# Two banks in two tiles: batch 0's numerators apart from their divisors, and another order of work

## The chip, the cores and the metric

The kernel runs on one core of one Trainium2 chip. The metric is device time in microseconds. The time before is 284.9 us, the median of three runs (284.8, 284.9 and 285.23).

## What is computed

The reference is a linear attention followed by a two-layer feed-forward block:

```python
# q, k, v: (8 batches, 8 heads, 576 positions, 64)
theta = pi / 2 * pos / 576
phi(x) = concat([relu(x) * cos(theta), relu(x) * sin(theta)], -1)   # 64 -> 128 features
q_p, k_p = phi(q), phi(k)
kv  = einsum('bhsf,bhsd->bhfd', k_p, v)          # 128 x 64 for each head
z   = sum(k_p, axis=2)                           # 128 for each head
num = einsum('bhsf,bhfd->bhsd', q_p, kv)
den = einsum('bhsf,bhf->bhs', q_p, z)[..., None] + 1e-06
x   = (num / den).transpose(0, 2, 1, 3).reshape(4608, 512)
h   = x @ w_in                                   # (512, 2048)
out = (relu(h) ** 2) @ w_out                     # (2048, 512) -> (4608, 512), float32
```

## The kernel before

Inputs are cast to bf16 as they are loaded. The 576 positions of a batch are cut into four blocks of 128 (j = 0 to 3) and a tail of 64 (j = 4). The tails of all eight batches are gathered and make up a ninth unit of the feed-forward block, so there are units u = 0 to 8: unit u is batch u, and unit 8 is the tails.

**Attention of a batch b.** `features` makes the feature rows of k and q (operations kf, qf, kqf). `values` copies v beside a column of ones (vc, vct), so that one product gives kv and z together. `kv` sums over the positions into the two banks of psA (operations kz), and the result is copied to `kvz` (8 heads x 65 columns, the 65th being z). q's features are transposed, by TensorE for batches 0 to 2 (tq, copied out by tqc), by a DMA for the others (qT on SyncE's queue). `numerators` multiplies q's transposed features with kvz (num): 8 products of 65 columns, four heads in each of two banks. Then den adds 1e-6 to the 65th column of each head, and div takes its reciprocal on VectorE and multiplies the 64 others with it, reading PSUM. x is transposed, by TensorE for batches 0 to 2 (tx, txc) and by DMA for the others (xT).

**Feed-forward of a unit u.** Units 0 and 1 do the first product plainly (G, evicted by a relu r, squared by sq), unit 0 the second one too (H, evicted by y0). From unit 2 on (from unit 1 on in the second product) a product of 2 x 2 blocks is done as seven products with sums of blocks in place of eight. In the first product (`first_seven`, four parts i for each unit) they are called P1 to P7 and go to the banks X, Y and E; their evictions are c1, cu and cv (copies of partial results), r11 and r21 (relu on either engine), and r22 and r12 (add and relu, line 829, always VectorE). In the second product (`second_seven`, and `last_seven` for unit 8) they are Q1 to Q7 and go to the banks X2, Y2 and E2: Q1 and Q2 sum in X2; Q5 and Q3 in E2; Q6, Q7 and Q4 in Y2. Between them stand the evictions d1 (X2 copied to Y2), y11 (out of X2), du and dv (out of Y2), y22 (E2 plus a part kept aside, line 961, VectorE), y21 (out of Y2), y12 (E2 plus another part, line 961). The sums of blocks of g (s1 to s4, `gsums`) and of x (t1 to t4) are VectorE's. One operation P or Q is four matmuls of 256 columns.

**PSUM.** There are eight banks of 512 float32 a partition. X, Y, E and Y2 are a tile each. psA is one tile of two banks, and so is psB, whose halves are called X2 and E2:

```python
bank = {n: psum.tile([P, FP], F32, name="ps" + n) for n in ("X", "Y", "E", "Y2")}
psA = psum.tile([P, 2, FP], F32, name="psA")
psB = psum.tile([P, 2, FP], F32, name="psB")
bank["X2"], bank["E2"] = psB[:, 0, :], psB[:, 1, :]
```

Batch 0's numerators alternate between the pairs psB (j = 0 and 2) and psA (j = 1 and 3); all later numerators go to psA. The transposes tq0.0 and tq0.2 go to X2 and E2, tq0.1 and tq0.3 to X and Y; those of batches 1 and 2 to psA.

**The order.** `plan.add` registers 1405 operations with keys of what they read and write; X2 and E2 have separate keys there. `TABLE` lists the operations by number, in the order in which they are issued; each engine runs its own in that order. A "+" gives an operation to the second engine that it may run on (of VectorE and ScalarE), and "a<b" holds the load a until operation b is done. The framework puts in the semaphores between engines by the tiles that an instruction reads and writes. `FILL` gives the sizes of groups of matmuls on zeros, into bank E, that stand in the opening: 11, 1, 4 and 1 (operations 1401 to 1404), besides 28 such matmuls at the start (warm). Loads are issued by GpSimd's queue, stores and DMA transposes by SyncE's.

Of the kernel before, what the change touches and what calls it, by code (L numbers as in the profile page):

```python
# [11 lines left out]
F32 = mybir.dt.float32  # L12
# [3 lines left out]
FP = 512  # L16
# [76 lines left out]
FILL = (11, 1, 4, 1)  # L93
TABLE = """
# [9 lines left out]
212 206+ 211 248 213 214 243 276 249 284 283 278+ 286 215 254 216 279 244+ 318<279 239 255 288  # L104
285+ 250 319<244 289 294 287 320<289 291 292+ 298 240+ 261 295+ 251+ 299+ 290 245 360 300+ 293+
357 257 362 321<357 301 297 219 364 303+ 302 296+ 224 246 322<302 247+ 304 323<224 230 306
324<304 305 225 325<305 307 326<225 226+ 252 309+ 308 361 220 253 363 256+ 310 259 311 365 312
313 258+ 314 221 315 260+ 316 262 263 227 317+ 476+ 266 479 480 474+ 477 233 475 473 264 234 478
265+ 267+ 495<478 327 270 328 329 272 271 332 273 235 333 486 334 485+ 236 483 484 337 481 237
268 366 338+ 339 330 269 231 359 274+ 342 335 331 487 371 343 344 372 373 232 368 374 336+ 340  # L110
347 482+ 345 348 381 349 375 488 496<348 382 341+ 369 383 497<382 346+ 350 489 498<350 351+ 490
409 491 413 410 499<409 492 412 414 493 358 376 500<412 494 418 411 501<358 416 370 419 384 417
502<416 420 385 415 503<420 421 504 428 422 423 386 505 424 506 425 429 377 426 378 507 427 431
508+ 433 432 387 509 434 388 389 367 510 435 390 627 443 436 631 430 633 630+ 511 629 438 437
391 439 392 512 635 628 444 440 513 393 640 394 632 448 395 441 514 446 449 396 379 447 515 450
516 380 403 451 397 442 517 634+ 445 453 452 458 454 649<442 518 636 398 639 459 637 399 650<398
638+ 463 651<399 461 519+ 464 455 652<461 520 404 462 456 465 653<404 643 457+ 466+ 644 654<643
645 646 655<466 460 468 467 567 656<468 469 563 405 568 564 406 657<405 565 470 566 572 471 647
# [4 lines left out]
788 612 671 606 538 613 672 787 533 791+ 539 803<787 615 609 616 551 550 617 673 674 552 618 553  # L123
534+ 675 721 792 619 790 789 557 620 793 717 804<789 554 718 797 805<554 555 622 720 798 610
806<622 623 558 559 611 722 807<610 560 614 808<560 799 621 726 724 719 727 624 561 725 800 625
728 562 736 729 556 626 801 723 795 802 731 676 679 732 680 737 681 796 730 682 678 812 683 739
733 740 813 741 814 694 742 695 734 696 735 743 815 744 738 809<815 751 816+ 817 746 810<751 684
747 745 811<746 685 818 752 686 677 687 819 688 754 820 821 756 697 757 755+ 748 698 822 749 758
823+ 699 824 759 689 936+ 753 944 825 942 761 941 943+ 766 937 826 762 938 690 950 760 691 767
692 827 750+ 940 763 828 771 935 769 764 948 700 772 770+ 701 702 693 773 703 875 774 704 833  # L130
768 939 776 775 949 705 777 946 706 947 876 871 778 872 711 945+ 779 712 957<711 713 765 780+
714 958<713 880 959<714 874 707 873 878 960<707 881 708 830 879 951 961<708 952 709 882 962<952
831 953 883 954 955 963<954 890 956 832 885 964<890 877 886 966 715 834 891 835 884 967+ 716 836
968 895 965<836 837 893 896 887 894 843 888 969 897 970 889+ 971 892 838 898+ 844 972 848 899
# [34 lines left out]
def kernel(  # L169
# [9 lines left out]
    nc = tc.nc  # L179
# [22 lines left out]
    psum = ctx.enter_context(tc.tile_pool(name="psum", bufs=1, space=bass.MemoryType.PSUM))  # L202

    def sb(name, shape, dt=BF16):
        return const.tile(shape, dt, name=name)


    bank = {n: psum.tile([P, FP], F32, name="ps" + n) for n in ("X", "Y", "E", "Y2")}
    psA = psum.tile([P, 2, FP], F32, name="psA")
    psB = psum.tile([P, 2, FP], F32, name="psB")  # L210
    bank["X2"], bank["E2"] = psB[:, 0, :], psB[:, 1, :]

    def as_bf(ap, n):

# [80 lines left out]
    def pe(t):  # L295
        return [("PE", t, t)]
# [242 lines left out]
    def numerators(b, j, banks="A"):  # L539
        src = qpT[j // 2][:, j % 2] if j < J else qptT  # L540
        kz = kvz[b % 2]

        ps, key = (psA, [("A",)]) if banks == "A" else (psB, [("X2",), ("E2",)])

        def mm():
            for hh in range(HH):
# [696 lines left out]
```

## Time and profile before

| | |
|---|---|
| median of the runs | 284.9 us |
| the profiled execution | 286.38 us |
| its span, first to last instruction | 284.6 us |
| mean granted TensorE clock | 0.997 |
| TensorE busy | 271.1 us, 2904 matmuls recorded |
| VectorE busy | 223.2 us, 430 instructions |
| ScalarE busy | 180.4 us, 290 instructions |
| DMA, mean over the span | 132 GB/s; the loads of batch 7 land by 177 us |

TensorE's busy time counts a matmul until its modelled end, which overlaps the start of the next: four matmuls of 256 columns are recorded with 0.60 us, and the next four start 0.436 us after them. A row of the timeline gives the start, the length, the engine, the line, what is written and read, the number of instructions, and in brackets the idle time of the engine before it and what ended that. Both banks of psB carry the name psB there.

### The profile page before, as it was taken

How to read it: one execution, taken by the hardware profiler on the slowest of the kernel's cores; microseconds unless marked ns; L12 is line 12 of the kernel's file. 1: busy time of each engine (PE TensorE's matmuls, PEld its weight loads, DVE VectorE, ACT ScalarE, POOL GpSimd, SP SyncE). 2: the span in 40 equal slices, each digit the busy share in tenths (PEclk: the TensorE clock that was granted, in tenths of full speed). 3: DMA queues.
4: the chain of work that ended last, by engine and by line, in shares of the span. 5: the costliest groups of instructions: out<-in, count | busy, mean ns of one | idle time of the engine just before them, and what ended most of it. 6: DMA issues, size and time to landing. Idle time of an engine off the chain costs nothing.

```text
span 284.6 us, 7089 instructions
## 1 busy us (share of the span) xinstructions
PE 271.1 (95%) x2904; PEld 228.7 (80%) x2911; DVE 223.2 (78%) x430; ACT 180.4 (63%) x290; POOL 58.8 (21%) x89
## 2 busy tenths in 40 slices
PE   8999999999899999999999999999999899999992
PEld 2579767867679798889897989799888788888882
DVE  0766888968889869999999879969779766776941
ACT  3756767789766787775577865755556368745220
POOL 8924164441070080014020530000000000000000
PEclk9999999999999999999999999999999999999998
DMA  8999989996979599999999799544321020300134
GB/s 190 188 207 191 196 112 180 202 175 117 198 97 153 111 111 224 212 182 120 267 129 150 114 176 156 112 85 167 114 39 74 2 84 2 147 2 0 76 109 114
DMA packets 82416, 37.62 MB, mean 132 GB/s; under 512 B 51664, under 2 KB 80336, under 8 KB 82384
## 3 DMA queue, kind: packets, MB, share of 16 engines
q0 software_dynamic: 42240, 17.83, 51.5%
q1 hardware_dynamic: 39504, 18.81, 27.6%
q10 hardware_dynamic: 640, 0.52, 0.7%
q8 instruction: 23, 0.38, 0.5%
q14 instruction: 9, 0.07, 0.1%
HBM read 36.70 MB, written 9.44 MB: 162 GB/s over the span
## 4 chain that ended last, share of the span: by engine, by line
PE 80%; DVE 12%; ACT 4%; issue 2%; DVEq 0%
PE psB L940 16%; PE psY L787 10%; PE psY L940 10%; PE psE L787 7%; PE psX L787 7%; PE psB L891 4%; PE psX L733 3%; PE psA L470 3%; PE psE L733 3%; PE psA L554 3%; PE psY L733 2%; PE psY L1014 2%; DVE rt L829 2%; PE psX L1093 2%; PE psE L1093 2%
## 5 line engine op out<-in xcount | busy, mean ns | idle before, releaser
L940 PEld LDWEIGHTS <-gT 128*128 128x128 bf16 x448 | 42.8, 98 | 8.5 <-issue 3.6
L787 PEld LDWEIGHTS <-w 128*128 128x128 bf16 x448 | 42.6, 98 | 4.8
L940 PEld LDWEIGHTS <-gs 128*128 128x128 bf16 x336 | 32.6, 98 | 6.4 <-issue 2.6
L787 PEld LDWEIGHTS <-w1s 128*128 128x128 bf16 x336 | 32.3, 98 | 3.8
L787 PE MATMUL psX<-xT,w 128*128 128x256 bf16 x224 | 33.6, 273 | 0.0
L787 PE MATMUL psY<-ts,w 128*128 128x256 bf16 x224 | 33.6, 273 | 0.0
L940 PE MATMUL psB<-w,gT 128*128 128x256 bf16 x224 | 30.4, 273 | 2.6 <-DVE ysb L961 1.8
L704 ACT ACTIVATE gT<-rt 128x2048 bf16<-128x2048 bf16 x15 | 28.7, 1911 | 5.6 <-DVE rt L829 5.4
L698 ACT ACTIVATE rt<-psY 128x512 bf16<-128x512 f32 x33 | 19.7, 597 | 16.4 <-PE psY L787 13.5
L702 DVE TENSOR_TENSOR gT<-rt 128x2048 bf16<-128x2048 bf16 x21 | 25.7, 1223 | 1.6 <-ACT rt L698 0.4
L733 PEld LDWEIGHTS <-w 128*128 128x128 bf16 x320 | 25.3, 98 | 2.0
L829 DVE CUSTOM_DVE_ANT_0 rt<-psE,p1u 128x512 bf16<-128x512 f32 x28 | 19.2, 686 | 8.5 <-PE psE L787 8.4
L698 ACT ACTIVATE rt<-psX 128x512 bf16<-128x512 f32 x34 | 20.4, 601 | 7.4 <-PE psX L787 3.7
L829 DVE CUSTOM_DVE_ANT_0 rt<-psE,p1v 128x512 bf16<-128x512 f32 x28 | 19.2, 687 | 6.9 <-PE psE L787 3.4
L571 DVE TENSOR_TENSOR x<-psA,rden 128x512 bf16<-128x512 f32 x30 | 20.7, 691 | 1.9
L336 POOL DMA_DIRECT2D kqin<-in_k_dram x7 | 6.5, 922 | 71.8 <-ACT psY L399 19.2
L399 ACT COPY p1v<-psY 128x512 f32<-128x512 f32 x24 | 14.1, 586 | 10.5 <-PE psY L787 10.4
L399 ACT COPY p1u<-psY 128x512 f32<-128x512 f32 x23 | 13.5, 586 | 9.4 <-PE psY L787 9.4
L399 ACT COPY psY<-psX 128x512 f32<-128x512 f32 (+1 forms) x27 | 15.2, 563 | 4.4 <-DVE rt L696 2.7
L940 PE MATMUL psB<-w2t,gs 128*128 128x256 bf16 x112 | 15.5, 273 | 1.7 <-DVE psY L399 0.8
L787 PE MATMUL psE<-ts,w1s 128*128 128x256 bf16 x112 | 16.8, 273 | 0.0
L787 PE MATMUL psE<-xT,w1s 128*128 128x256 bf16 x112 | 16.8, 273 | 0.0
(153 smaller groups left out, 550.0 us busy)
## 6 DMA issues: line engine op xcount, KB each, us to landing
out_dram<-ysb SPq DMA_DIRECT2D x16, 512.0 KB, 3.5
kqin<-in_q_dram POOLq DMA_DIRECT2D x8, 512.0 KB, 7.5
kqin<-in_k_dram POOLq DMA_DIRECT2D x7, 512.0 KB, 6.5
vin<-in_v_dram POOLq DMA_DIRECT2D x7, 512.0 KB, 7.6
w<-in_moe_w_in_dram POOLq DMA_DIRECT2D x4, 512.0 KB, 11.7
w<-in_moe_w_out_dram POOLq DMA_DIRECT2D x4, 512.0 KB, 9.6
ysb<-in_k_dram SPq DMA_DIRECT2D x1, 1024.0 KB, 5.7
kqint<-in_k_dram POOLq DMA_DIRECT2D x16, 32.0 KB, 5.5
```

Source lines behind the costliest of these rows:

```text
L399: (nc.vector.tensor_copy if e == "DVE" else nc.scalar.copy)(out=dst, in_=src)
L470: nc.tensor.matmul(out=psA[:, half, hh * E1 : (hh + 1) * E1], lhsT=lhsT, rhs=rhs, start=(j == 0 and hh == 0), stop=(j == js[-1] and hh == ...
L571: nc.vector.tensor_tensor(out=x.rearrange("p (b k) (l d) -> p b k l d", b=n, l=2), in0=n4[:, :, :, 0:D].rearrange("p b (k l) d -> p b k l ...
L698: nc.scalar.activation(out=dst, in_=src, func=ACTF.Relu)
L702: nc.vector.tensor_tensor(out=dst, in0=src, in1=src, op=ALU.mult)
L704: nc.scalar.activation(out=dst, in_=src, func=ACTF.Square)
L733: nc.tensor.matmul(out=bank[bk][:, hh * W + c0 : hh * W + c1], lhsT=w1[:, kb, (h0 + hh) * P : (h0 + hh + 1) * P], rhs=x_block(u, t, kb)[:, ...
L787: nc.tensor.matmul(out=acc[:, hh * W : (hh + 1) * W], lhsT=lhs[:, kk, c : c + P], rhs=rhs(kk), start=start and hh == 0 and kk == 0, stop=T ...
L829: nc.vector._custom_dve(dve_ops.TENSOR_ADD_SAT, out=dst, in0=wide(acc), in1=wide(part), s0=INF, s1=0.0)
L891: nc.tensor.matmul(out=bank[bk][:, :], lhsT=g[:, hb, tt_ * P : (tt_ + 1) * P], rhs=w2[:, hb, :], start=(hb == 0), stop=True, skip_group_ch ...
L940: nc.tensor.matmul(out=acc[:, pr * W : (pr + 1) * W], lhsT=lhs[:, hb, pr * P : (pr + 1) * P], rhs=rhs[:, hb, :], start=start and pr == 0 a ...
L1093: nc.tensor.matmul(out=bank[("X", "E")[i % 2]][:, :], lhsT=zeros[:, 0:P], rhs=zeros[:, :], start=True, stop=True,)
```

## The change

X2 and E2 become tiles of their own, like the other banks, and psB is gone. Batch 0's numerators j = 0 and 2 are laid out otherwise: X2 holds the 8 x 64 numerators and E2 the 8 divisors, by 16 products in place of 8 (`mm_apart`, with the heads in order 0 to 7; before, heads 0, 4, 1, 5 and so on). den reads E2 alone, and div reads X2 alone. The planner's cost of these two operations is set to 0.5 us. The first fill has 8 matmuls in place of 11, the second 2 in place of 1, the third stays at 4, and the fourth is gone. The table of order is a new one of 1404 operations: nearly every operation is at another place, 133 of them (features, evictions, squares, dens) change between VectorE and ScalarE, and 38 of the 45 held loads are held by another operation.

```diff
-FILL = (11, 1, 4, 1)
+FILL = (8, 2, 4)
 TABLE = """
-0 1 2 3 4 6 5 7 8 9 24 10 17 22+ 25 19 23+ 11 20 12 16+ 18+ 13 21+ 14 1401 29 33+ 39 15 44 28+
-43 38 26 34 30 50 27 35 32+ 48 87 1402 37 31+ 51 52 36+ 53 40 49 88 41+ 42 54 55 45 56 57+ 46+
...
+0 1 2 3 4 6 5 7 8 9 10 17+ 19 18 22+ 25 11 21 12 16+ 23 20 24+ 13 14 1401 33+ 34 29 15 38 43+ 39
+35 28 26 44+ 30 37 27 36 50+ 1402 48 32+ 87 31+ 51 52 53 40 49 88 41+ 42 54 55 45 56 57+ 46+ 58
...
-    bank = {n: psum.tile([P, FP], F32, name="ps" + n) for n in ("X", "Y", "E", "Y2")}
+    bank = {n: psum.tile([P, FP], F32, name="ps" + n) for n in ("X", "Y", "E", "X2", "Y2", "E2")}
     psA = psum.tile([P, 2, FP], F32, name="psA")
-    psB = psum.tile([P, 2, FP], F32, name="psB")
-    bank["X2"], bank["E2"] = psB[:, 0, :], psB[:, 1, :]
...
-        ps, key = (psA, [("A",)]) if banks == "A" else (psB, [("X2",), ("E2",)])
+        key = [("A",)] if banks == "A" else [("X2",), ("E2",)]
...
+        def mm_apart():
+
+            for h in range(H):
+                for dst, cs in (
+                    (bank["E2"][:, h : h + 1], slice(D, E1)),
+                    (bank["X2"][:, h * D : (h + 1) * D], slice(0, D)),
+                ):
+                    nc.tensor.matmul(out=dst, lhsT=src[:, h, :], rhs=kz[:, h, cs], start=True, stop=True)
...
-        add(f"num{b}.{j}", pe(0.243 if j < J else 0.251), lambda e: mm(), rd, key, at=at_att(b, NUM0 + NUM1 * j))
+        go, t = (mm, 0.243 if j < J else 0.251) if banks == "A" else (mm_apart, 0.5)
+        add(f"num{b}.{j}", pe(t), lambda e: go(), rd, key, at=at_att(b, NUM0 + NUM1 * j))
...
-        n4 = ps[:, 0:n, 0 : HH * E1].rearrange("p b (h e) -> p b h e", e=E1)
+        if banks == "A":
+            n4 = psA[:, 0:n, 0 : HH * E1].rearrange("p b (h e) -> p b h e", e=E1)
+            nx, nd = n4[:, :, :, 0:D], n4[:, :, :, D]
+        else:
+            nx = bank["X2"][:, :].rearrange("p (b h e) -> p b h e", b=n, e=D)
+            nd = bank["E2"][:, 0:H].rearrange("p (b h) -> p b h", b=n)
```

More of the change, by code (lines that the diff above doesn't have):

```diff
@@ L92 @@
 ORDER2 = 'kvq23'
-FILL = (11, 1, 4, 1)
+FILL = (8, 2, 4)
 TABLE = """
[9 rows of a table removed]
[L104 to L118, printed above, removed]
[4 rows of a table removed]
-788 612 671 606 538 613 672 787 533 791+ 539 803<787 615 609 616 551 550 617 673 674 552 618 553
-534+ 675 721 792 619 790 789 557 620 793 717 804<789 554 718 797 805<554 555 622 720 798 610
@@ L125 @@
[L125 to L134, printed above, removed]
[26 rows of a table removed]
[9 rows of a table added]
+206+ 248 211 279+ 213 214 243 249 281 282 215 360 254 244 278 216+ 283 284+ 250 318<278 288 289+
+239 291 319<288 292 293+ 251+ 320<292 298 295+ 240+ 257 300+ 290 294 299+ 245 255+ 321<294 286+
@@ new lines @@
+301 246+ 287+ 261 303+ 285 296 302+ 219 297 362 322<297 247+ 304 364 323<362 252 306 324<364 361
+224 258 325<252 363 305+ 220 365 253+ 307 326<365 230 309+ 256 308+ 259 221 262+ 310 260 263 311
+312 313 314 315 478 316 266 477 481+ 476 317 233 473 479 267 474 234 264 480 265+ 475 327 272
+495<475 328 329 270 366 332 271 235 333 486 334 483+ 236 273 337 237 268 338 339 485+ 335 269
+330 359 371 274+ 342 331 231 343 487 344 225 336+ 368 372 232 373 226 340 345 484 482+ 347 227
+367 374 341+ 381 488 496<374 348 349 346+ 382 497<381 369 375 383 350 498<382 489 351+ 490 491
@@ new lines @@
+409 413 499<491 410 492 358 414 376 500<492 377 412 501<358 411 418 370 416 419 502<418 493 384
+417 503<493 420 494 385 415 421 504 386 505+ 422 423 506 428 424 425 429 387 426 388 433 427 507
+434 431 389 508 432 509 435 390 443 630 436 510 511 628 430 512+ 629 438 631 391 439 627 392 513
+640 444 393 394 437 448 395 632 514 446 449 633 440 396 515+ 447 450 516 397 451 398 441 517 378
+453 442 458 454 445 634 459 403 452 649<634 404 636+ 638 463 635+ 637 518 639 455 464 519
+650<639 520 399 461 651<399 456 465 462+ 652<461 457+ 379 466+ 405 653<462 460 380+ 643 654<460
@@ new lines @@
+468 467 567 655<468 469 563 406 564 568 644 656<406 470 566 565 645 657<566 572 407 570 573 471
[4 rows of a table added]
+534 607 609 608 671 551 610 613 552 787 553 789+ 793 617 792 803<787 791+ 790 538 618+ 615
+804<538 550 679 616 805<618 619 539 614 806<619 620 672 721 621 673+ 807<539 622 717 554 808<621
+623 718 557 720 722 624 674 558 611+ 625 559 675 726 626 797 724 795 727 798 799 719 725 800 801
+560 802 728 561 723 729 736 555 730 812 731 813+ 556 680 814 732 796 733 737 681 676 682 562 741
+683 815 678 739 742 684 816+ 740 809<739 743 677 689 744 810<743 690 734 691 811<690 746 735 751
[3 rows of a table added]
@@ L161 @@
+768 945+ 875 871 827 776 947 775 707 777 828 833 876 872 778 708 874 873 880 709 779 712 957<880
+881 713 780 714 958<713 882 959<714 878 830 883 951 960<878 952 879 953 954 832 955 961<954 885
+956 962<955 890 886 831 877 963<832 966 891 834 967+ 884 835 964<966 836 715 895 965<836 837 968
[27 rows of a table added]
 """
@@ L547, in mm @@
                 for half in range(2):
-                    e0 = hh * E1
+                    h, e0 = half * HH + hh, hh * E1
                     if j < J:
-                        dst, lhsT = ps[:, half, e0 : e0 + E1], src[:, half * HH + hh, :]
+                        dst, lhsT = psA[:, half, e0 : e0 + E1], src[:, h, :]
                     else:
                         p0, p1 = half * TAIL, (half + 1) * TAIL
-                        dst, lhsT = ps[p0:p1, 0, e0 : e0 + E1], src[:, hh, p0:p1]
-                    nc.tensor.matmul(
-                        out=dst, lhsT=lhsT, rhs=kz[:, half * HH + hh, :], start=True, stop=True
-                    )
+                        dst, lhsT = psA[p0:p1, 0, e0 : e0 + E1], src[:, hh, p0:p1]
+                    nc.tensor.matmul(out=dst, lhsT=lhsT, rhs=kz[:, h, :], start=True, stop=True)
+        def mm_apart():
[5 more added lines that the diff above has]
+                    nc.tensor.matmul(out=dst, lhsT=src[:, h, :], rhs=kz[:, h, cs], start=True, stop=True)
         rd = [("qpT", j), ("qpT", j, 0), ("qpT", j, 1), ("kvz", b % 2)]
@@ L572, in div @@
                 out=x.rearrange("p (b k) (l d) -> p b k l d", b=n, l=2),
-                in0=n4[:, :, :, 0:D].rearrange("p b (k l) d -> p b k l d", l=2),
+                in0=nx.rearrange("p b (k l) d -> p b k l d", l=2),
                 in1=rd_[:, 0:n]
@@ L581, in plus_eps @@
         def plus_eps(e):
-            src = n4[:, :, :, D]
+            src = nd
             if e == "DVE":
```

78 rows, old and new, of the table TABLE are left out of this document.

## The prediction

> **What bounds the kernel now.** I read the page's first and fourth parts, then the stretches, then the tile view of psB, then the timeline of each place where TensorE stood still.
>
> ```profile
> PE 271.1 (95%) x2904; PEld 228.7 (80%) x2911; DVE 223.2 (78%) x430; ACT 180.4 (63%) x290; POOL 58.8 (21%) x89
> PE 80%; DVE 12%; ACT 4%; issue 2%; DVEq 0%
> 120.00:140.00 20.00, 20.00 (x230) 17.66 (x229) 19.06 (x36) 13.94 (x21) 4.27 (x6) 1.00 1.09 193
> ```
>
> TensorE (PE) carries 80% of the chain that ended last. In the third line (a stretch of 20 us; busy PE, PEld, DVE, ACT, POOL) PE never idles although VectorE (DVE) works 19.06 of 20 us. So the time is PE's work plus PE's pauses, and a pause is worth its full length. The tile view of psB says who ends pauses before its instructions:
>
> ```profile
>   DVE ysb L961: 2.6, 5
>   ACT psY L399: 1.3, 3
>   ACT ysb L399: 1.1, 3
>   DVE psY L399: 0.8, 1
> ```
>
> L961 is y12 and y22, which read bank E2; psY L399 is d1 and ysb L399 is y11 or y0, most of which read X2. Next to the order of work, the timeline shows which bank PE was about to write:
>
> ```profile
> 155.19 0.69 DVE L961 TENSOR_TENSOR ysb<-psB,p2v 128x512 f32<-128x512 f32 x1
> 155.94 0.60 PE L940 MATMUL psB<-w,gT 128*128 128x256 bf16 x4 [0.53 <-DVE ysb L961]
> ...
> 222.01 0.70 DVE L399 COPY psY<-psB 128x512 f32<-128x512 f32 x1 [0.26 <-PE psB L940]
> 222.76 0.60 PE L940 MATMUL psB<-w2t,gs 128*128 128x256 bf16 x4 [0.79 <-DVE psY L399]
> ...
> 269.30 0.60 PE L1014 MATMUL psB<-w,gT 128*128 128x256 bf16 x4
> 269.93 0.69 DVE L961 TENSOR_TENSOR ysb<-psB,p2u 128x512 f32<-128x512 f32 x1 [0.29 <-PE psB L1014]
> 270.68 0.60 PE L1014 MATMUL psB<-w,gT 128*128 128x256 bf16 x4 [0.78 <-DVE ysb L961]
> ```
>
> At 155.94 PE wants to write X2 (Q1 of unit 4) and waits for y22 of unit 3, which reads E2. At 222.76 it wants E2 (Q5 of unit 6) and waits for d1, which reads X2. At 270.68 Q2 of unit 8 goes on in X2 and waits for y12 of unit 7 in E2; and that y12 had itself waited for a Q2 into X2. The plan has separate keys, ("X2",) and ("E2",), so none of these waits is in the plan. They exist because both banks lie in the one tile psB.
>
> **The waits that go.** There are eleven such pauses. Their idle times as shown are 0.67 (at 76.96), 0.66 (79.46), 0.37 (95.94), 0.24 (97.21), 0.53 (155.94), 0.40 (165.91), 0.53 (182.61), 0.24 (207.92), 0.79 (222.76), 0.09 (261.44) and 0.78 (270.68): 5.30 us. A group of four products is recorded with 0.60 us, but the next group starts 0.436 after it where nothing waits, so each pause also costs the 0.164 of overlap: 11 x 0.164 = 1.80. Together 7.10 us. For each I looked up what the plan itself demands of that bank (for Q1 at 155.94 the y11 before it, for Q2 at 270.68 its d1, which ended at 268.59): all of it had ended before PE paused. So nothing takes the place of these waits in the old order; bounds 6.0 (should two of the longer ones meet another wait) to 7.10. I take 7.10.
>
> **Batch 0's numerators.** num0.0 and num0.2 become 16 products each: eight of 64 columns into X2, eight of 1 column into E2, each with its own weight load. No row shows a 128x1 product. The nearest are 128x65 at 29 ns from start to start and the 64-row 64x65 ones at 17 ns, so 16 cost 0.27 to 0.46 us against 8 x 0.029 = 0.23. I take 0.46, from the row with the same 128x128 weight load: +0.23 each. num0.0 hides it:
>
> ```profile
> 15.34 0.38 ACT L399 CAST kvz<-psA 128x260 bf16<-128x260 f32 x1
> 15.81 0.42 DVE L399 CAST kvz<-psA 128x260 bf16<-128x260 f32 x1
> 16.69 0.17 DVE L584 TENSOR_SCALAR den<-psB 128x8 f32<-128x8 f32 x1 [0.46 <-PE psB L554]
> 17.13 0.69 DVE L571 TENSOR_TENSOR x<-psB,rden 128x512 bf16<-128x512 f32 x1
> 18.04 0.69 DVE L571 TENSOR_TENSOR x<-psA,rden 128x512 bf16<-128x512 f32 x1
> ```
>
> Now products of both halves alternate, and the second one waits for the second kvz copy (16.23); seven follow it. In the new loop the heads of half 0 come first, ready at 15.72, and eight of the 16 remain after 16.23: 0.23 instead of 0.20. num0.2 (18.11) runs while DVE divides j=1 (18.04 to 18.73) and num0.3 waits for that anyway, so its +0.23 is covered; a fill that stood behind it is gone (-0.22). The second kvz copy starts late because the copy ahead of it on DVE waited 1.28 us for ScalarE's copy out of the other psB bank. That wait goes, but the two kvz copies both read psA, which stays one tile, and in this trace two engines reading one pair tile go one after the other: 15.72 at the earliest instead of 15.81, 0.09 less. den and div keep 8 and 512 elements per partition. Fills: 17 to 14, 3 x 0.216 = 0.65 us of PE work in places where PE waits; nothing on the path. Of the first fill the work behind it takes 0.65, but the first kz product needs vc0, which now stands on DVE behind both tqc0.1 copies: it ends near 13.4 by adding rows, where kz0.0 now starts at 13.38. Opening together: -0.05 us; bounds -0.5 (both kvz copies at once) to +0.6 (both numerators exposed and vc0 late).
>
> **The new order.** It moves almost every operation a little. I added PE's work along both lists, at the trace's durations (265.6 us before, 265.4 after), and read off how much of it stands between a bank's last product, its eviction and its next product. The shortest such lead in the stage of units 2 to 8 is 0.87 us in both lists (but for one txc at 0.72 in both), and the rows at 0.87 did not pause before. Loads: k, q, v of batches 3 to 7 have 8.0 us or more of PE work between gate and first use; q7 is the tight one, 8.8 where it took 9.1 from issue to landing, worth at most 0.3 us on DVE. SyncE's queue: the puts and transposes change places, but each x transpose keeps at least 3.1 us to its first reader, the tail of batch 7, which landed in 2.4. DVE is the tight engine. The new list puts 38.9 us of DVE work beside the 40 us of PE work from 60 to 100 and 38.6 beside 140 to 180 (record times summed, times 223.2 / 245.7 for their overlap). The busiest stretch seen without a pause is 19.06 of 20. If DVE can't be fuller than that, these two need 40.8 and 40.5: +1.3 us. If it can, nothing. I take the middle, +0.7. The four pauses of 0.3 to 0.4 us at tq1 (psA) stay.
>
> **The sum.** 286.38 (the profiled execution; span 284.6 and 1.8 around it) - 7.10 - 0.05 + 0.70 = 279.9. The median of the runs shown lies 1.48 below that execution, so the forecast is 278.5 us.
>
> **Rivals.** (a) DVE gives back more: with no pauses of PE to catch up in, the evictions r12, r22, y12, y22 and the divisions fall behind in units 2 to 6. For it: 97% in two stretches. Against it:
>
> ```profile
> DVE rt L829 <- PE psE L787: 11.8, 14, 2.5
> ```
>
> DVE stood waiting for PE before 14 of its 56 add-and-relu evictions, so it is not behind as a rule. If a third to a half of the 7.1 comes back: 281 to 282.2. Chance 0.14.
>
> (b) The same mechanism, but as the new bound, ends slower: there are 28 units of seven products, each with r22 and r12 on DVE ahead of a product that needs their bank. The gain is gone when each unit pauses PE for 7.1 / 28 = 0.25 us on average; at 0.3 us it is 8.4, and 277.8 (the sum without the 0.7) + 8.4 = 286.2. Chance 0.06.
>
> (c) The split does not do what it says: what the waits guard is needed, or another wait stands right behind each. Then 284.9 within 0.5. Against it are the plan's keys and the readers that had ended. psX, psY and psE, separate tiles, are written and read at the same time all through the trace. The Trainium skill says the same as a rule (PSUM — Partial Sum Buffer, "PSUM bank collisions raise a hardware error"): two engines must not meet in one bank, while different banks run clean. By that rule too the cross-bank waits guard nothing. Chance 0.04.
>
> (d) TensorE's clock falls back in the opening, since three fills are gone. The first twelve warm-up products took 0.43 us from start to start and later ones 0.216: half speed for some 5.3 us from the start. A second such ramp costs half of that, 2.6: 281.1. The largest idle time I get in the opening is 0.5 us, and the 0.79 at 222.76 left the clock as it was. The Trainium skill (TensorE: Matmul & The Clock Gate, "Part 1: The HAM clock gate") has the clock halve after an idle window of about 3.4 us; by it this doesn't happen. Chance 0.03.
>
> **Chances and range.** Forecast as worked out: 0.73, 276.8 (277.8 without new waits, less 0.45 for the opening at its best, less 0.55 of tq1's pauses) to 280.3 (6.0 saved, +1.3, +0.6). The range reaches into (a) and (d): 276.8 to 282.0. A measurement of this kernel tells about 0.2% (0.6 us) from no change. Faster: 0.73 + 0.14 + 0.03 + 0.01 of (c) = 0.91; within: 0.03; slower: 0.06.
>
> **What would show it.** After the change the psB tile is gone. No product into X2 should wait for y12 or y22, and none into E2 for y11 or d1; PE's idle time between 75 and 272 us falls from 5.3 us to under 1; num0.0 starts near 15.9 and the first G0 product near 19.3, now 19.34; what follows PE's last product (5.0 us to the end) stays. The forecast is wrong if PE shows new waits on rt L829 or x L571 that sum to over 2 us, or if the waits in psX2 and psE2 remain.

## The result and the profile after

The changed kernel takes 280.57 us, the median of six runs (280.11 to 281.82), beside 285.06 (284.46 to 285.88) for the kernel before: a ratio of 0.985, with a 95% interval of 0.9819 to 0.988. The profiled execution took 280.15 us, its span is 278.4. In the chain of work that ended last, TensorE's share has grown from 80% to 85%, and VectorE's has fallen from 12% to 4%. The page of the changed kernel (busy time of each engine; the chain by engine; one group of products of the second stage, whose last column is the idle time before it), and then the same group on the page of the kernel before:

```profile
PE 268.7 (97%) x2917; PEld 228.3 (82%) x2924; DVE 227.0 (82%) x427; ACT 176.7 (63%) x293; POOL 58.8 (21%) x89
PE 85%; DMA 6%; DVE 4%; issue 1%; ACT 1%; POOL 1%; POOLq 0%; DVEq 0%
...
L951 PE MATMUL psX<-w,gT 128*128 128x256 bf16 x224 | 30.7, 273 | 0.0
```

```profile
L940 PE MATMUL psB<-w,gT 128*128 128x256 bf16 x224 | 30.4, 273 | 2.6 <-DVE ysb L961 1.8
```

The group at L951 is Q1 and Q2 into X2 (the profile leaves out the 2). Its idle time is 0.0; before, the same products into psB had 2.6 us. None of the eleven cross-bank pauses is left, and TensorE's idle time between 75 and 272 us has fallen from 5.3 us to 1.1, all of it in two new pauses. New is a 6% share of DMA in the chain. Two rows of TensorE's timeline show the two new pauses, one of which ends with a DMA (start, length, what is written and read, idle time before and its releaser):

```profile
88.71 0.40 PE L552 MATMUL psA<-kvz,qpT 128*128 128x65 bf16 x8 [0.22 <-DVE x L582]
116.86 0.42 PE L552 MATMUL psA<-kvz,qpT 128*128 128x65 bf16 x8 [0.89 <-DMA qpT<-kqp]
```

The first is num3.2, which waits for div3.1; with the overlap of 0.164 it costs 0.38 us. The second is num4.2, which waits for a DMA transpose of q's features; it costs 1.05. SyncE's queue shows why that came late:

```profile
105.67 0.33 SPq L877 DMA_DIRECT2D out_dram<-ysb  x1
106.11 6.02 SPq L503 DMA_TRANSPOSE qpT<-kqp  x1
```

The transpose stands behind a store that had to wait until 105.67. It was issued only then, took 6.0 us to issue, beside the loads of batch 5, and landed at 116.81, 10.7 us after its start. TensorE took up num4.2 at 116.86; without the pause it would have done so at 115.81, 9.7 us after the issue.

The kernel before has the same transpose behind the same kind of store, with less time ahead of its reader, and there TensorE didn't pause (SyncE's queue, then num4.2):

```profile
110.28 4.30 SPq L505 DMA_TRANSPOSE qpT<-kqp  x1
```

```profile
118.58 0.41 PE L554 MATMUL psA<-kvz,qpT 128*128 128x65 bf16 x8
```

It landed at 118.26, 8.0 us after its start and 0.3 us before num4.2. So the place behind a store alone doesn't make the pause: it is the place together with a landing that took 2.7 us longer.

For the accounts below I use one stretch that is free of the opening and of the tail: from the start of the first G0 product to the start of TensorE's last product. It is 259.97 us before and 254.55 after, 5.4 less.

### The profile page after: what moved, and what is told of

The parts are those of the page before. It is cut to its first block, busy times and chain, and to the rows that moved or that the text cites. A ratio compares the mean times of both kernels' runs of the same rounds, so it can differ in the third digit from the quotient of the medians.

```text
span 278.4 us, 7126 instructions
## 1 busy us (share of the span) xinstructions
PE 268.7 (97%) x2917; PEld 228.3 (82%) x2924; DVE 227.0 (82%) x427; ACT 176.7 (63%) x293; POOL 58.8 (21%) x89
## 3 DMA queue, kind: packets, MB, share of 16 engines
HBM read 36.70 MB, written 9.44 MB: 166 GB/s over the span
## 4 chain that ended last, share of the span: by engine, by line
PE 85%; DMA 6%; DVE 4%; issue 1%; ACT 1%; POOL 1%; POOLq 0%; DVEq 0%
PE psY L798 12%; PE psY L951 12%; PE psE L798 8%; PE psE L951 8%; PE psX L798 8%; PE psX L951 8%; DMA qpT<-kqp 4%; PE psA L468 4%; PE psX L744 3%; PE psA L552 3%; PE psE L744 3%; PE psY L744 3%; DMA kqin<-in_q_dram 2%; PE psX L902 2%; PE psY L1025 2%; PE psA L524 1%
## 5 line engine op out<-in xcount | busy, mean ns | idle before, releaser
L951 PEld LDWEIGHTS <-gT 128*128 128x128 bf16 x448 | 43.1, 98 | 5.3
L951 PEld LDWEIGHTS <-gs 128*128 128x128 bf16 x336 | 32.4, 98 | 3.8
L713 DVE TENSOR_TENSOR gT<-rt 128x2048 bf16<-128x2048 bf16 x24 | 29.4, 1224 | 4.1 <-ACT rt L709 2.0
L951 PE MATMUL psX<-w,gT 128*128 128x256 bf16 x224 | 30.7, 273 | 0.0
L709 ACT ACTIVATE rt<-psY 128x512 bf16<-128x512 f32 x34 | 20.3, 598 | 16.1 <-PE psY L798 14.6
L715 ACT ACTIVATE gT<-rt 128x2048 bf16<-128x2048 bf16 x12 | 22.8, 1911 | 4.2 <-DVE rt L840 3.9
L397 ACT COPY psY<-psX 128x512 f32<-128x512 f32 (+1 forms) x35 | 19.6, 560 | 7.2 <-PE psX L1025 3.0
L709 ACT ACTIVATE rt<-psX 128x512 bf16<-128x512 f32 x31 | 18.6, 601 | 6.9 <-PE psX L798 5.5
L397 ACT COPY p1v<-psY 128x512 f32<-128x512 f32 x23 | 13.5, 586 | 12.7 <-PE psY L798 12.6
L798 PE MATMUL psY<-ts,w1s 128*128 128x256 bf16 x112 | 16.8, 273 | 0.0
## 6 DMA issues: line engine op xcount, KB each, us to landing
w<-in_moe_w_in_dram POOLq DMA_DIRECT2D x4, 512.0 KB, 10.7
```

The costliest lines, as they stand in the source:

```text
L397: (nc.vector.tensor_copy if e == "DVE" else nc.scalar.copy)(out=dst, in_=src)
L709: nc.scalar.activation(out=dst, in_=src, func=ACTF.Relu)
L713: nc.vector.tensor_tensor(out=dst, in0=src, in1=src, op=ALU.mult)
L715: nc.scalar.activation(out=dst, in_=src, func=ACTF.Square)
L798: nc.tensor.matmul(out=acc[:, hh * W : (hh + 1) * W], lhsT=lhs[:, kk, c : c + P], rhs=rhs(kk), start=start and hh == 0 and kk == 0, stop=T ...
L951: nc.tensor.matmul(out=acc[:, pr * W : (pr + 1) * W], lhsT=lhs[:, hb, pr * P : (pr + 1) * P], rhs=rhs[:, hb, :], start=start and pr == 0 a ...
```

## The experiments

**The split alone: new tiles, old table, old fills.**

```diff
-FILL = (8, 2, 4)
-TABLE = <new>
+FILL = (11, 1, 4, 1)
+TABLE = <old>
```

> The change with the old table of order and the old fills: only the tiles are split and batch 0's numerators laid out apart. Theory 1 (the waits across the pair's banks cost PE 7.1 us and nothing stands behind them): none of the eleven pauses is left, PE's other pauses stay below 1 us after 76 us, and the time is 5 to 7 us under before, 278 to 280. Rival (the new order did it): the pauses move to other operations on X2 and E2, and the time is within 1.5 us of before, 283.5 to 285.

Measured: 278.38 us beside 285.22, a ratio of 0.9769 (0.9725 to 0.9814). The stretch is 253.04, 6.93 under before. After 60 us TensorE pauses nowhere; busy time by stretch (length, then busy PE, PEld, DVE, ACT, POOL) of this kernel, and of the kernel before:

```profile
60.00:100.00 40.00, 40.00 (x469) 33.39 (x467) 36.06 (x78) 31.86 (x50) 10.18 (x16) 1.00 1.05 142
100.00:140.00 40.00, 40.00 (x464) 35.57 (x463) 36.92 (x65) 27.86 (x44) 8.56 (x13) 1.00 1.24 189
140.00:180.00 40.00, 40.00 (x435) 35.65 (x433) 37.55 (x73) 30.23 (x48) 8.54 (x12) 1.00 1.13 158
180.00:220.00 40.00, 40.00 (x429) 35.59 (x428) 33.37 (x55) 23.07 (x35) 0.00 (x0) 1.00 0.30 85
```

```profile
60.00:100.00 40.00, 37.96 (x444) 31.19 (x445) 35.45 (x75) 29.92 (x46) 8.13 (x13) 1.00 0.95 139
140.00:180.00 40.00, 39.08 (x431) 34.77 (x429) 36.34 (x68) 27.81 (x45) 8.55 (x12) 1.00 1.05 148
```

Theory 1 holds: with the same order of work, what disappears is the waits, and nothing stands behind them. VectorE gets 0.6 and 1.2 us fuller in the two stretches that are shown for both kernels and delays nothing. The rival (the order did it) is out.

**The order alone: old tiles, new table, new fills.**

```diff
+FILL = (8, 2, 4)
+TABLE = <new>
```

> The kernel before with the new table and the new fills, psB still one tile. Theory 1: the new list has cross-bank pairs of its own (17 by the plan's keys, among them Q1 after y12 or y22 and Q5 after d1), so pauses of 0.2 to 0.9 us each stand before products into psB, 5 to 8 us in all, and the time is 284 to 288, not under before by more than 1 us. Rival (the order): 280 to 282, as after the change.

Measured: 283.52 beside 285.22, a ratio of 0.9929 (0.9901 to 0.9957), so 0.5 us better than the theory's best. The new list has cross-bank waits of its own. The tile view of psB gives who ended the idle time of any engine before its instruction (us and times):

```profile
  DVE ysb L961: 3.5, 4
  ACT psY L399: 0.9, 2
  ACT ysb L399: 0.7, 1
  DVE psY L399: 0.3, 1
```

The first line holds 2.4 us of ScalarE's own waits. TensorE's pauses before products into psB, in its timeline, are 0.68 (at 75.92), 0.71 (79.34), 0.22 (110.86), 0.57 (128.75), 0.07 (168.03), 0.53 (211.51) and 0.27 (221.47); with the overlap of 0.164 each, these seven cost 4.2 us, less than the 5 to 8 expected and than the 7.10 of the old list. num4.2 pauses 0.88 for its transpose here too. So the new order suffers less from the pair than the old one does, but the pair still costs it most. The two halves of the change do not add up: the split is worth 6.8 us with the old order, and 3.6 with the new one (283.52 to 279.93, the changed kernel measured beside these).

**The changed kernel again**, measured together with these two.

> The changed kernel once more, for its median beside the other three and for a second look at the opening. Theory on the spread between executions (half-speed warm-up products last 3.7 us in one profile and 6.3 us in another): if this profile has fewer half-speed products than six, or as many, its span is near 278.4; with twelve, its opening is 0.6 to 0.9 us later and its span 279 to 280. Rival (the spread comes from DMA landings later on): spans that differ while the opening is the same.

Measured: 279.93 us (ratio 0.9812, 0.9785 to 0.9839); its stretch is 254.47, as in the first profile. Its median is 1.55 over that of the split with the old table, and its pauses account for that: 0.96 at num4.2, 0.38 at num3.2 and 0.17 at a P7, start to start. Nine products of the warm-up ran at half speed here, against seven in the first profile. The first G0 product still started at 18.63, not later than 18.73. So the expectation's steps were too coarse; the table in the next section has all the profiles.

**The transpose ahead of the stores.** Only the place of operation 641 (qT4.1) moves.

```diff
-... 445 634 459 ...  648 641 577 ...
+... 445 634 641 459 ...  648 577 ...
```

> The changed kernel with one move in its table: the second DMA transpose of batch 4's features goes ahead of unit 1's two stores and two other operations on SyncE's queue, right behind the last feature that it reads. Theory (num4.2 paused 1.05 us because this transpose was issued at 106.1, behind the store, into batch 5's loads, and took 10.7 us to land): it is issued near 97, the pause of 1.05 us before num4.2 is gone, and the time is 0.7 to 1.1 us under the changed kernel in the same call. Rival (the DMA engines are full there whenever it is issued, or PE then waits for something else 1 us later): under 0.3 us.

Measured: 279.03, 0.90 under the changed kernel measured beside it; the stretch is 253.52, 0.95 shorter. The timeline of SyncE's queue, and then TensorE's at num4.2:

```profile
97.67 1.75 SPq L503 DMA_TRANSPOSE qpT<-kqp  x1
```

```profile
115.85 1.04 PE L951 MATMUL psY<-w2t,gs 128*128 128x256 bf16 x8
116.72 0.41 PE L552 MATMUL psA<-kvz,qpT 128*128 128x65 bf16 x8
```

Issued at 97.67, it takes 1.75 us to issue in place of 6.02, lands at 103.88, 6.2 us after its start in place of 10.7, and num4.2 follows its predecessor without a pause. So this pause goes when the transpose leaves its place behind the store, and the rival (full DMA engines at any time) is out. Whether the store or the loads beside it stretched the issue and the landing, this move doesn't separate.

**num3.2 later, on top of that.**

```diff
-... 436 510 511 628 430 512+ ...
+... 436 510 628 430 511 512+ ...
```

> The changed kernel with the early transpose of batch 4's features and one more move in its table: num3.2 goes behind P5.2.1 on TensorE, 0.44 us later. Theory (the new table's cost under the split is these two waits and little else): the pause of 0.38 us before num3.2 is gone, the stretch from the first G0 product to the last product is 253.1 to 253.3 us (253.5 with the first move alone, 254.5 with neither, 253.04 with the old table), and the time is within 0.5 us of the split with the old table. Rival (other parts of the new order cost too): the pause is gone but the stretch stays at 253.5 or the time stays 0.6 us or more over the split with the old table.

Measured: 279.45 beside 279.09 for the split with the old table, measured with it. The pause before num3.2 is gone, but the stretch is 254.07, not 253.2: three pauses stand elsewhere in this profile (0.25 and 0.30 us at tq2.0 and a G1 near 52 us, 0.38 at a P3 at 174.9). The first two are not in the profile of the kernel without this move, at a place that the move comes well after, so they differ between executions; the third may be the move's own. The median is within the 0.5 us expected, the stretch is not, so this one settles nothing beyond the pause itself.

**The split with the old table again.**

> The split with the old table and the old fills once more, as the base of the other three in this call. Its pauses after 60 us were none in the first look; the same is expected, with 252.9 to 253.2 us from the first G0 product to the last product of TensorE, and a time near 278.4.

Measured: 279.09 beside 285.15 (ratio 0.9783, 0.9748 to 0.9818), 0.7 over the first median; no pause after 60 us, and a stretch of 252.90. The split alone is thus worth 6.1 us here and 6.8 in the first measurement.

**A version that beats both: batch 1's transposes in two pairs.** The four pauses at tq1 were left in every kernel so far. On the split with the old table:

```diff
-                q_transpose_pe(b, j, "A")
+                q_transpose_pe(b, j, ("X2", "E2") if b == 1 and j % 2 else "A")
```

> The split with the old table, and the transposes j = 1 and 3 of batch 1's features go to X2 and E2 in place of psA, so that two pairs alternate. Theory (the four pauses of 0.31 to 0.42 us at tq1 are there because the copies of both halves of psA go one after the other and the next transpose needs both): they are gone, 1.58 us, and the time is 1.2 to 1.6 us under the split with the old table. Rival (the copies and features on VectorE and ScalarE are the limit there): the pauses move to num1, kz1 or H0 and the time falls by less than 0.6 us.

Measured: 277.48 beside 285.15, a ratio of 0.9733 (0.9691 to 0.9774), and 1.6 under the base. TensorE's timeline of the base, then of this kernel:

```profile
31.43 0.61 PE L524 MATMUL psA<-ident,kqp 128*128 128x128 bf16 x8
31.87 1.04 PE L744 MATMUL psX<-xT,w 128*128 128x256 bf16 x8
33.17 0.61 PE L524 MATMUL psA<-ident,kqp 128*128 128x128 bf16 x8 [0.26 <-DVE qpT L397]
```

```profile
30.87 1.04 PE L744 MATMUL psX<-xT,w 128*128 128x256 bf16 x8
31.74 0.61 PE L524 MATMUL psA<-ident,kqp 128*128 128x128 bf16 x8
...
35.92 1.13 PE L468 MATMUL psA<-vx,kqp 128*128 128x65 bf16 x32 [0.22 <-DVE qptT L397]
```

In the base, transposes start 1.74 us apart with 1.32 us of work; now the transposes follow the G0 product ahead of them at once. One pause of 0.38 comes up at kz1.0 behind the last copy, so of 1.58 us 1.2 are saved there; the stretch is 251.86, 1.04 shorter. The rest of the 1.6 between the medians isn't traced to the change: the runs of the two kernels overlap (276.4 to 280.16 and 278.31 to 280.37).

**Five matmuls fewer in the first fill, on top of that.**

```diff
-FILL = (11, 1, 4, 1)
+FILL = (6, 1, 4, 1)
```

> The kernel with the two pairs alternating, and the first fill has 6 products in place of 11. Theory (the fill ends after the data are there only where the half-speed warm-up is long): with 13 or 14 half-speed products the first G0 product starts up to 1 us earlier than 19.6, with 7 to 9 it does not move from 18.5 to 18.8; the median falls by 0 to 0.6 us. Rival (with fewer fills TensorE's clock falls back): half-speed products again after 11 us and a time 1 us or more higher.

Measured: 277.19 (ratio 0.9708, 0.9676 to 0.974), 0.3 under, less than the two ranges tell apart. The profile caught seven half-speed products; the first G0 product starts at 18.52, where the kernel with 11 fills and as many half-speed products has 18.21. TensorE idles 1.34 us before tq0.0, and the clock stays: the 128-column products right behind that pause start 56 ns apart, as everywhere later. So in this execution the five matmuls were neither the limit of the opening nor needed for the clock; whether they cost something when the warm-up is long wasn't caught. In this profile num4.2 pauses 0.85 us for its transpose with the old table, too. The transpose was issued 8.3 us before TensorE was ready for num4.2, as in tq_two, and took 9.1 us to land, where it took 6.7 in tq_two. So that lead is thin in the old order too, and the landing differs between executions.

## Why the prediction was right, and where it was off

**The waits that go: right.** 7.10 us were worked out from eleven pauses; the split alone takes 6.93 off the stretch, and 6.84 and 6.06 off the median in two measurements. The reading that the tile, not the plan, made the waits was the whole of it.

**Batch 0's numerators and the opening: right.** The new products start 26 to 29 ns apart; 15 of these steps and the last make 0.43 us for 16, against the 0.46 taken. In num0.0 the eight of half 0 run ahead of the second kvz copy, which again waits 0.40 us for ScalarE's copy out of the other half of psA, as foreseen:

```profile
15.17 0.43 DVE L397 CAST kvz<-psA 128x260 bf16<-128x260 f32 x1 [0.40 <-ACT kvz L397]
```

With 14 half-speed products in the warm-up (the table below has all the profiles) the first G0 product starts at 19.64 with the new table and fills (qt_early) and at 19.61 with the old ones (split_old): no difference, where -0.05 was forecast. In qt_early kz0.0 pauses 0.47 for a vc0 copy, which stands behind the copies of tqc0.1, so the three fills saved return nothing. The numerators alone cost nothing either: split_old has them, the kernel before doesn't, and from the end of the warm-up to the first G0 product it is 9.42 and 9.44 us. With only seven half-speed products the new opening starts G0 at 18.73 and the old one (tq_two) at 18.21, 0.5 later in one profile each, still within the bounds of -0.5 to +0.6.

**The new order: the size was off, and the reason given was not the cause.** +0.7 was taken, from VectorE's load. Measured are +1.5 (254.5 against 253.0). The load that the term was built on, 38.9 and 38.6 us beside 40 us of TensorE's work, didn't come: from 60 to 100 us VectorE works 35.2 us, and from 140 to 180 the changed kernel has

```profile
140.00:180.00 40.00, 40.00 (x436) 35.80 (x435) 37.56 (x68) 29.30 (x48) 7.97 (x12) 1.00 1.05 165
```

with 40.00 of 40 us of TensorE. That is 94%, under the 95% that the term took for the limit, so over 40 us that limit was not put to the test. Over 20 us it is passed:

```profile
90.00:110.00 20.00, 20.00 (x224) 17.62 (x223) 19.44 (x36) 14.22 (x24) 6.46 (x9) 1.00 1.02 142
```

VectorE works 97% here, and TensorE doesn't pause. What cost was order in two queues: a division behind a square on VectorE (0.38), and the transpose behind a store on SyncE (0.96 to 1.05). The step of the prediction that failed is the sentence on SyncE's queue: it checked the leads of the x transposes to their readers, and left out q's. qT4.1 had 9.7 us of TensorE's work between its issue and num4.2, and needed 10.7. Looking the lead up would not have been enough: by the 8.0 us that the same transpose took in the kernel before, 9.7 is plenty. Behind the store it took 6.7 to 9.1 us to land in the five profiles of the old order, and 10.6 to 10.9 in the three of the new one (the changed kernel twice, and pair_new). Why it takes longer there stays open.

**From the profiled execution to the median: off by 1.9 us.** The prediction took 1.48 us off because before's median lay that far under its profile. The changed kernel's median lies 0.42 over its profile. Before's profile happened to have a long warm-up. All the profiles, by the number of warm-up products at half speed (0.43 us apart, then 0.216):

| half-speed products | kernel | warm-up ends, us | first G0 product, us |
|---|---|---|---|
| 7 | the changed kernel | 8.58 | 18.73 |
| 7 | tq_two | 8.61 | 18.21 |
| 7 | tq_fill | 8.66 | 18.52 |
| 8 | qt_num | 8.85 | 18.66 |
| 8 | pair_new | 8.87 | 18.50 |
| 9 | after_again | 9.07 | 18.63 |
| 11 | split_old2 | 9.56 | 18.98 |
| 13 | before | 9.90 | 19.34 |
| 14 | split_old | 10.19 | 19.61 |
| 14 | qt_early | 10.19 | 19.64 |

Up to nine the opening doesn't follow the warm-up; beyond, it starts up to 1 us later, with either table and either set of fills. Before's profile had 13 and the changed kernel's 7. So the difference between these two profiles (6.2 us) flatters the change by 0.6 in the opening, and the offset of 1.48 belonged to one execution, not to the kernel. That the number of half-speed products sets the spread between runs is argued from these ten profiles; it was not set by hand, and it is not the whole: the opening explains some 0.6 of the 1.48, and the profile of tq_fill, with seven, lies 1.07 over its median, 0.85 of it in the pause at num4.2.

The terms together: against the profiles the forecast of 279.9 was 0.2 too low (0.2 less saved by the split and 0.8 more for the order, against 0.6 less in the opening and 0.2 less behind TensorE's last product), and against the medians the conversion adds 1.9; that is the 2.1 us between 278.5 and 280.57.

**The range.** 280.57 lies above the 280.3 up to which the forecast's own working was said to reach, and inside the range only as it was widened for (a) and (d), which didn't happen. The three bounds named for that end add up to 280.8, not 280.3 (284.9 - 6.0 + 1.3 + 0.6); but they aren't what happened either, as the split saved nearly all of its 7.10. The mechanism was right; that the time fell into the range owes something to the room left for rivals.

**The rivals.** (a), VectorE gives back a third to a half, came nearest in size (281 to 282.2; half of 7.1 on top of 278.5 is 282.05), but of its cause only the 0.38 at a division shows. (b) didn't happen; in the same trace VectorE still stood waiting for TensorE before 14 of its 56 add-and-relu evictions. (c) is refuted by the split alone. (d), a second half-speed ramp, is in none of these profiles: behind the warm-up, products of 128, 256 and 512 columns start 56, 109 and 216 ns apart in all ten, and no run of them at twice that.

## What to carry to other kernels

A wait that the plan doesn't contain is found by setting the releaser's bank against the bank that the waiting product writes; where they differ, look for a tile that spans both, and give each bank its own before anything is reordered. Test a new order apart from such a repair: here the repair alone was worth 6.1 to 6.8 us, and the new table that came with it gave 1.5 back. When leads are checked in a moved list, every queue's every kind of transfer counts, with some room for a landing that takes longer than the one on record, and an offset between one profile and a median isn't carried over before the opening of that profile is looked at.

## What the hardware showed that was not expected

The length of the half-speed start varies between executions of like programs from 7 to 14 products, so that the switch comes 3.9 to 7.2 us after the span's start. The Trainium skill (TensorE: Matmul & The Clock Gate, "Part 1: The HAM clock gate") says that the window that releases the clock runs freely, that the switch therefore moves by about 500 ns either way, and that one kernel had 6, 11 or 14 slow products from run to run. The 7 to 14 of these rows agree with the last of these; the spread of 3.3 us is wider than the second. The granted clock in the profile's rows doesn't show this start (the changed kernel, the figure behind POOL's):

```profile
0.00:4.00 4.00, 2.81 (x7) 1.04 (x8) 0.38 (x5) 1.68 (x3) 2.81 (x11) 1.00 0.39 117
```

It is 1.00 there, while the products start 0.43 us apart; the distance between products tells it.

A DMA transpose of the same size took 1.75 us to issue and 6.2 to land at 97.7 us, and 6.02 and 10.7 at 106.1, behind a store and beside loads; in the old order, at that place, it took 4.3 to 6.4 to issue. Neither time is a constant of the instruction.
